# Tile 0's second matrix product: chunks 8 to 15 in three float32r products where plain float32 stood

## The chip, the cores and the metric

The kernel runs on one core of one Trainium2 chip. The metric is the device time in microseconds (us) of one execution. A core has five engines that each work through their own queue in order: PE (TensorE, matrix products, with weight loads counted apart as PEld), DVE (VectorE), ACT (ScalarE), POOL (GpSimd) and SP (which issues the transfers here).

## The reference

```
x = attention(q, k, v)        # 4 batches x 8 heads x 576 rows x 64, window of 128, slopes by head
h = x @ moe_w_in              # 2304 x 512 times 512 x 2048
r = max(h, 0)
g = s * (r * r) + b
y = g @ moe_w_out             # 2304 x 2048 times 2048 x 512
a, c = y @ moe2_w1, y @ moe2_w2
out = ((a * c) @ moe2_w3) @ moe2_w_out
```

## The kernel before

The 2304 rows are cut into six tiles of 384 (`TT`), and the hidden width of 2048 into sixteen chunks of 128 (`NC1`). For each tile and chunk the kernel makes the first product into `hp` (`mlp_h`), takes relu and square on ACT into `r` (`mlp_relu`, `mlp_g`), and adds the second product, chunk by chunk, into four accumulators `acc` (`mlp_x`, one per 128 output columns). Attention runs one head per slot beside it, some heads ahead: scores `s` on PE, mask and minimum `ns` on DVE (L311, then L320), exponentials on ACT (L334), their sums `sm` on DVE (L344, L345), normalizing `pr` on POOL (L347), a transpose `tp` on PE (L368), the split of it `pp` on ACT and DVE (L380, L381), a selection `pt` on POOL (L384), and the product with the values, `pv`, on PE (L421).

Two ways of multiplying are used. Tiles 1 to 5 use float32r, with each operand split into a high part and the rest: an operand x becomes xh = round(x) and xl = x - xh, and a product is three products, high by high, high by rest, rest by high (`PASSES`). Tile 0 uses plain float32 operands without a split, in both products of the first layer (L482 and L534). A plain float32 product is one instruction in the program and two rows in the trace: L534 has 64 in the program (16 chunks of 4) and 128 in the trace. A float32r product is one row.

The weights arrive as 8-byte numbers and are decoded by `decode`: ACT reads the upper words into a scratch tile `z` (L98), DVE does a shift and two merges (L100, L103, L109). The scratch pool has two buffers. With `plain` the last merge writes the finished weight `wz` to a tile of its own and so frees `z`; without it the merge writes into `z`, and ACT and POOL then split `z` into the two halves of a weight tile `w` (L121, L122). All 32 weight chunks of the first layer (16 of w_in, 16 of w_out, by turns) are decoded plain before and during tile 0. Those of tile 0 that are plain are split afterwards for tiles 1 to 5: `mlp_x` puts them on the list `unsplit`, and `split_some` takes four in each slot from slot 7 on (`weight_split`: ACT copy L131, subtraction L132 on POOL and on DVE by turns). The pool of weight tiles has 33 buffers for 32 chunks, so such splits follow each other through one spare buffer.

The order in which each engine meets its instructions is set when the program is built: the framework's scheduler starts from the order of the source and moves instructions by a timeline of its own, engine by engine. On the chip each engine's queue is then strictly in order.

Of the kernel before, what the change touches and what calls it, by code (L numbers as in the profile page):

```python
# [8 lines left out]
F32 = mybir.dt.float32  # L9
F32R = mybir.dt.float32r  # L10
U32 = mybir.dt.uint32
BF16 = mybir.dt.bfloat16
AF = mybir.ActivationFunctionType
ALU = mybir.AluOpType
# [7 lines left out]
P = 128  # L22
TT = 384
# [9 lines left out]
EARLY = H  # L33
EX = 2
AHEAD = 3
PASSES = ((0, 0), (0, 1), (1, 0))


@with_exitstack
def kernel(  # L40
    ctx: ExitStack, tc: tile.TileContext, qk0, qk, v, relm, w_in, w_out, s, b, w1, w2, w3T, wo2, qsc, v0, out
):
    nc = tc.nc
# [3 lines left out]
    wp = ctx.enter_context(tc.tile_pool(name="wp", bufs=2 * NC1 + 1))  # L47
    xp = ctx.enter_context(tc.tile_pool(name="xp", bufs=2 * KD))
    gp = ctx.enter_context(tc.tile_pool(name="gp", bufs=2))
# [36 lines left out]
    def decode(raw, pool, tag, done, free=None, plain=False):  # L86

        z = zp.tile([P, DM], F32, tag="z", name="z")  # L90
        if raw.dtype == F32:
            nc.vector.tensor_copy(out=z, in_=raw)
            yield
        else:
            zu = z.bitcast(U32)
            wu = raw.bitcast(U32).rearrange("p (n t) -> p n t", t=2)
            wf = raw.bitcast(F32).rearrange("p (n t) -> p n t", t=2)
            nc.scalar.activation(out=z, in_=wf[:, :, 1], func=AF.Copy, scale=2.0 ** -112)  # L98
            yield
            nc.vector.tensor_scalar(  # L100
                out=zu, in0=zu, scalar1=3, scalar2=None, op0=ALU.logical_shift_left
            )
            nc.vector.scalar_tensor_tensor(  # L103
                out=zu, in0=wu[:, :, 1], scalar=0x80000000, in1=zu,
                op0=ALU.bitwise_and, op1=ALU.bitwise_or,
            )
            if plain:
                z = pool.tile([P, DM], F32, tag=tag, name="wz")
            nc.vector.scalar_tensor_tensor(  # L109
                out=z.bitcast(U32), in0=wu[:, :, 0], scalar=29, in1=zu,  # L110
                op0=ALU.logical_shift_right, op1=ALU.bitwise_or,
            )
            if plain:
                done(z)
                yield
                return
        if free:
            free()
        yield
        w = pool.tile([P, 2, DM], F32R, tag=tag, name="w")  # L120
        nc.scalar.activation(out=w[:, 0, :], in_=z, func=AF.Copy)  # L121
        nc.gpsimd.tensor_tensor(  # L122
            out=w[:, 1, :], in0=z, in1=w[:, 0, :].bitcast(F32), op=ALU.subtract
        )
        done(w)
        yield
# [64 lines left out]
    def load_raws(n):  # L191
        for _ in range(n):
            if nraw[0] < len(raws):
                raw_load(*raws[nraw[0]])
                nraw[0] += 1

    def tick(n=1):
        for _ in range(n):
            if todo:
                need[0] += 1  # L200
                if len(raws) == 2 * NC1 and need[0] + AHEAD > nraw[0]:
                    load_raws(need[0] + AHEAD - nraw[0])
                flight.append(todo.pop(0)())
# [267 lines left out]
    wi, wo, hps, gs, x2acc, unsplit = {}, {}, {}, {}, {}, []  # L471
# [6 lines left out]
    def mlp_h(t, c):  # L478
# [9 lines left out]
        n = 0  # L488
        for l, r in PASSES:
            for k in range(KD):  # L490
# [14 lines left out]
    def mlp_g(t, c):  # L505
        rt = gs[t, c]
        nc.scalar.activation(out=rt[:, :TT], in_=rt[:, :TT], func=AF.Square)
        if t == 0:
            nc.vector.memset(rt[:, TT:], 1.0)
            return  # L510
        gh = gp.tile([P, TT], F32R, tag="gh", name="gh")
        nc.scalar.activation(out=gh, in_=rt[:, :TT], func=AF.Copy)  # L512
        gs[t, c] = rt, gh

    def mlp_gl(t, c):
        if t == 0:
            return
        rt, gh = gs[t, c]
        gl = gp.tile([P, TT], F32R, tag="gl", name="gl")
        nc.vector.tensor_tensor(  # L520
            out=gl, in0=rt[:, :TT], in1=gh.bitcast(F32), op=ALU.subtract
        )
        gs[t, c] = gh, gl

    def mlp_x(t, c):
        g = gs.pop((t, c))
        w = TT + EX if t == 0 else TT
        if c == 0:
            for m in range(KD):
                x2acc[m] = ps_acc.tile([P, w], F32, tag="acc", name="acc")  # L530
        for m in range(KD):
            ms = slice(m * P, (m + 1) * P)
            if t == 0:
                nc.tensor.matmul(  # L534
                    out=x2acc[m], lhsT=wo[c][:, ms], rhs=g,
                    start=(c == 0), stop=(c == NC1 - 1),
                )
                continue
            for n, (l, r) in enumerate(PASSES):
                nc.tensor.matmul(  # L540
                    out=x2acc[m], lhsT=wo[c][:, l, ms], rhs=g[r],
                    start=(c == 0 and n == 0), stop=(c == NC1 - 1 and n == 2),
                )
        if t == 0:
            unsplit.extend(((wi, c), (wo, c)))
        if c == NC1 - 1:
            for m in range(KD):
                z = xp.tile([P, TT], F32, tag="x", name="ev")
                bm = bcol[:, m:m + 1]
                if t == 0:  # L550
                    nc.vector.tensor_scalar(
                        out=bm, in0=x2acc[m][:, TT:TT + 1], scalar1=b_sb[:, 0:1], scalar2=None,
                        op0=ALU.mult,
                    )
                if m % 2:
                    nc.vector.tensor_scalar(
                        out=z, in0=x2acc[m][:, :TT], scalar1=s_sb[:, 0:1], scalar2=bm,
                        op0=ALU.mult, op1=ALU.add,
                    )
                else:  # L560
                    nc.scalar.activation(
                        out=z, in_=x2acc[m][:, :TT], func=AF.Identity, scale=s_sb[:, 0:1], bias=bm
                    )
                nc.sync.dma_start(out=x2d[t][m], in_=z)
# [4 lines left out]
    def w3_unit(ig, j, accs):  # L569
# [3 lines left out]
        for i in range(4):  # L573
            for n, (l, r) in enumerate(PASSES):
                nc.tensor.matmul(  # L575
# [28 lines left out]
    def mlp2_ab(t, c):  # L604
        ps = []
        for w in (wa, wb):
            d = ps_rot.tile([P, TT], F32, tag="rot", name="ab")
            n = 0
            for l, r in PASSES:
                for k in range(KD):  # L610
# [19 lines left out]
    def mlp2_o(t, c):  # L630
        p = ps2.pop((t, c))
        for i in range(NB):
            if c == 0:
                oacc[i] = ps_acc.tile([P, DM], F32, tag="acc", name="acc")
            cs = slice(i * P, (i + 1) * P)
            for n, (l, r) in enumerate(PASSES):
                nc.tensor.matmul(  # L637
# [13 lines left out]
    for c in range(NC1):  # L651
        for d, src in ((wi, w_in[c]), (wo, w_out[c * P:(c + 1) * P, :])):
            raw = wp.tile([P, DM], src.dtype, tag="w", name="raw")
            raws.append((raw, src))
            todo.append(
                lambda raw=raw, d=d, c=c: decode(
                    raw, wp, "w", lambda w: d.__setitem__(c, w), plain=True
                )
            )
    att_load(0)  # L660
# [32 lines left out]
    def slot(n, m):  # L693
# [17 lines left out]
        if mlp:  # L711
            mlp_relu(*seq[1])
            mlp_g(*seq[1])
        if s1:
            att_min(n)
        if mlp:
            mlp_gl(*seq[1])
            pre_tick(more)
        if q > 0:
            mlp_x(*seq[0])  # L720
# [21 lines left out]
        if mlp:  # L742
            mlp_g(*seq[2])
            if v2 is not None:
                att_v(v2)
                att_x(v2)
            mlp_gl(*seq[2])
        if v2 is not None:
            att_xt(v2)
        if mlp:  # L750
            tick()
            pre_tick(more)
            mlp_x(*seq[1])
# [11 lines left out]
    n, m = EARLY, 0  # L765
# [44 lines left out]
    for m in range(KD):  # L810
        x2_split(0, m)
    mlp_x(NTILE - 1, NC1 - 1)
    accs = []
    while fresh[0] < npre[0]:
# [91 lines left out]
```

## Time and profile before

| | |
|---|---|
| time, median of 3 runs | 911.92 us (906.9 to 913.98) |
| the profiled execution's own time | 907.65 us |
| its span, first to last instruction | 905.9 us |
| mean granted TensorE clock | 0.990 of full speed |
| PE busy | 887.2 us (98%), 4833 rows |
| DVE, ACT, POOL busy | 484.6, 453.4, 340.4 us |

The profiled execution lies 4.3 us below the median, and 1.75 us of its time lie outside its span. PE is busy nearly throughout, so the questions are what PE has to do in the stretch that the change touches (about 60 to 190 us from the start of the span), and where in it PE waits.

### The profile page before, as it was taken

What the parts mean: (1) busy time and instruction counts of PE and PEld (TensorE: products, weight loads), DVE (VectorE), ACT (ScalarE), POOL (GpSimd) and SP (SyncE); (2) the same over time, 40 slices, a digit from 0 to 9 for tenths busy, and PEclk for the clock granted to TensorE, in tenths of its full rate; (3) what the DMA queues carried; (4) which work ended last, traced back from release to release, by engine and by line L of the source; (5) the groups of instructions that cost most, each with busy time, mean ns of one, the idle gap of its engine ahead of it and who ended that gap; (6) DMA issues with size and microseconds to landing.
All of it is one profiled execution on the core that took longest, in us unless ns stands there. A gap on an engine that the chain in (4) does not pass through costs nothing.

```text
span 905.9 us, 13384 instructions
## 1 busy us (share of the span) xinstructions
PE 887.2 (98%) x4833; PEld 805.5 (89%) x4836; DVE 484.6 (53%) x1012; ACT 453.4 (50%) x1052; POOL 340.4 (38%) x376
## 2 busy tenths in 40 slices
PE   8989989999999999999999999999999999999997
PEld 4756656999999999999999999899999999999996
DVE  5998866766688887788752621482211212121212
ACT  5756667776767787777754543342212121121211
POOL 0154687775567686777641301240101001010000
PEclk8989999999999999999999999999999999999999
DMA  8974211213334455445326962130201002000000
GB/s 312 304 283 166 100 64 46 85 59 112 99 127 166 169 201 170 145 157 181 117 94 224 385 261 84 56 116 1 71 1 35 36 1 70 1 36 1 35 1 36
DMA packets 37219, 104.38 MB, mean 115 GB/s; under 512 B 4512, under 2 KB 10656, under 8 KB 37152
## 3 DMA queue, kind: packets, MB, share of 16 engines
q1 hardware_dynamic: 37152, 103.52, 33.0%
q8 instruction: 38, 0.62, 0.3%
q14 instruction: 29, 0.24, 0.1%
HBM read 82.00 MB, written 21.50 MB: 114 GB/s over the span
## 4 chain that ended last, share of the span: by engine, by line
PE 85%; DVE 6%; issue 2%; POOL 2%; ACT 2%; DMA 2%; SPq 1%; DVEq 0%; ACTq 0%; POOLq 0%
PE ab L611 21%; PE acc L540 17%; PE hp L491 17%; PE acc L637 11%; PE hp L482 3%; PE acc L534 3%; PE pv L421 3%; PE w3a L575 2%; DVE z L103 2%; PE tp L368 1%; PE s L298 1%; PE s L297 1%; PE s L292 1%; DMA vraw<-v 1%; DVE z L100 1%
## 5 line engine op out<-in xcount | busy, mean ns | idle before, releaser
L611 PE MATMUL ab<-x,w 128*128 128x384 f32 x1152 | 208.3, 335 | 0.0
L611 PEld LDWEIGHTS ab<-x,w 128*128 128x128 f32 x1152 | 201.8, 188 | 4.3
L491 PE MATMUL hp<-x,w 128*128 128x384 f32 x960 | 186.2, 340 | 0.9 <-DVE pp L381 0.9
L540 PE MATMUL acc<-gh,w 128*128 128x384 f32 x640 | 177.3, 339 | 0.0
L491 PEld LDWEIGHTS hp<-x,w 128*128 128x128 f32 x960 | 167.6, 188 | 1.4 <-DVE pp L381 1.1
L625 DVE TENSOR_TENSOR a<-ab,a 128x384 f32<-128x384 f32 x48 | 26.7, 557 | 197.7 <-PE ab L611 179.8
L540 PEld LDWEIGHTS acc<-gh,w 128*128 128x128 f32 x640 | 115.3, 188 | 0.3
L540 PE MATMUL acc<-gl,w 128*128 128x384 f32 x320 | 108.6, 339 | 1.5 <-DVE gl L520 1.5
L599 POOL TENSOR_TENSOR x<-x,x 128x384 fp32r<-128x384 f32 x24 | 25.6, 1093 | 203.8 <-ACT x L598 191.9
L347 POOL TENSOR_SCALAR pr<-pr,sm 128x128 f32<-128x128 f32 x120 | 63.5, 543 | 88.3 <-DVE sm L345 34.7
L637 PE MATMUL acc<-w3o,ph 128*128 128x512 f32 x288 | 89.9, 394 | 0.0
L624 ACT ACTIVATE a<-ab 128x384 f32<-128x384 f32 x48 | 23.6, 492 | 131.7 <-PE ab L611 131.7
L259 POOL TENSOR_TENSOR kb<-qkraw,ka 128x512 fp32r<-128x512 f32 x40 | 56.2, 1404 | 71.4 <-ACT ka L258 71.3
L384 POOL TENSOR_SCALAR_AFFINE_SELECT pt<-pp 128x768 fp32r<-128x768 f32 x80 | 77.2, 986 | 7.0 <-PE pv L421 6.5
L520 DVE TENSOR_TENSOR gl<-r,gh 128x384 fp32r<-128x384 f32 x80 | 57.8, 723 | 33.6 <-ACT gh L512 32.4
L311 DVE CUSTOM_DVE_ANT_0 ns<-s,relm_sb 128x256 f32<-128x256 f32 (+1 forms) x144 | 52.9, 412 | 39.2 <-PE s L298 30.1
L626 ACT ACTIVATE ph<-a 128x384 fp32r<-128x384 f32 x48 | 25.2, 525 | 92.7 <-DVE a L625 92.7
L502 ACT ACTIVATE r<-hp 128x384 f32<-128x384 f32 x96 | 46.5, 486 | 49.6 <-PE hp L491 43.5
L540 PEld LDWEIGHTS acc<-gl,w 128*128 128x128 f32 x320 | 60.3, 188 | 2.3 <-DVE gl L520 2.2
L637 PEld LDWEIGHTS acc<-w3o,ph 128*128 128x128 f32 x288 | 53.4, 187 | 8.9
L637 PE MATMUL acc<-w3o,pl 128*128 128x512 f32 x144 | 56.5, 396 | 0.2 <-DVE pl L627 0.2
L334 ACT ACTIVATE pr<-pr,mn 128x128 f32<-128x128 f32 x120 | 46.8, 392 | 19.3 <-DVE pr L320 16.6
(89 smaller groups left out, 1423.4 us busy)
## 6 DMA issues: line engine op xcount, KB each, us to landing
qkraw<-qk SPq DMA_DIRECT2D x45, 448.0 KB, 3.3
late<-st SPq DMA_DIRECT2D x23, 512.0 KB, 3.4
w<-late SPq DMA_DIRECT2D x23, 512.0 KB, 7.1
raw<-w_in SPq DMA_DIRECT2D x16, 512.0 KB, 7.1
raw<-w_out SPq DMA_DIRECT2D x16, 512.0 KB, 6.7
raw<-w SPq DMA_DIRECT2D x16, 512.0 KB, 5.2
st<-w3T SPq DMA_DIRECT2D x15, 512.0 KB, 3.8
vraw<-v SPq DMA_DIRECT2D x20, 256.0 KB, 2.6
```

The source lines that it names most:

```text
L259: nc.gpsimd.tensor_tensor(out=kl, in0=k_r, in1=k.bitcast(F32), op=ALU.subtract)
L311: nc.vector.tensor_tensor_reduce(out=n[:, i, cs], in0=dst[i][:, cs], in1=relm_sb[:, VARIANT.get(t * NB + i, 0), cs], scale=2.0 ** -(h + 1) ...
L334: nc.scalar.activation(out=e[:, i, :], in_=e[:, i, :], func=AF.Exp, scale=-1.0, bias=mn[:, i:i + 1], accum_out=sm[:, i:i + 1],)
L347: nc.gpsimd.tensor_scalar(out=e[:, i, :], in0=e[:, i, :], scalar1=sm[:, i:i + 1], scalar2=1.0, op0=ALU.mult, op1=ALU.mult,)
L384: nc.gpsimd.affine_select(out=o[:, :, :, e, :], in_=pp.bitcast(F32), pattern=[[0, 2], [0, NB], [sign, P]], compare_op=op, fill=0.0, base=0 ...
L421: nc.tensor.matmul(out=d, lhsT=l, rhs=r, start=(n == 0), stop=(n == len(mms) - 1), skip_group_check=True)
L491: nc.tensor.matmul(out=hp, lhsT=wi[c][:, l, k * P:(k + 1) * P], rhs=xT[t, k][:, r, :], start=(n == 0), stop=(n == 3 * KD - 1),)
L502: nc.scalar.activation(out=rt[:, :TT], in_=hps.pop((t, c)), func=AF.Relu)
L520: nc.vector.tensor_tensor(out=gl, in0=rt[:, :TT], in1=gh.bitcast(F32), op=ALU.subtract)
L540: nc.tensor.matmul(out=x2acc[m], lhsT=wo[c][:, l, ms], rhs=g[r], start=(c == 0 and n == 0), stop=(c == NC1 - 1 and n == 2),)
L611: nc.tensor.matmul(out=d, lhsT=w[c][:, l, k * P:(k + 1) * P], rhs=x2[t, k][:, r, :], start=(n == 0), stop=(n == 3 * KD - 1),)
L637: nc.tensor.matmul(out=oacc[i], lhsT=p[l][:, cs], rhs=w3o[c][:, r, :], start=(c == 0 and n == 0), stop=(c == NC2 - 1 and n == 2),)
```

## The change

For tile 0 a constant `PLAIN = 8` parts the second product. Chunks 0 to 7 stay as they were. For chunks 8 to 15 the weight of w_out is decoded with its split at once (L121 and L122 of `decode`, on ACT and POOL), the squared activations are split into `gh` and `gl` as in the other tiles (ACT L512, DVE L520, now 386 columns wide with the two columns of ones), and the second product is made of three float32r products. These eight weight chunks no longer go on the list `unsplit`, which therefore holds 24 entries and not 32.

```diff
+PLAIN = 8
@@ mlp_g
         if t == 0:
             nc.vector.memset(rt[:, TT:], 1.0)
-            return
-        gh = gp.tile([P, TT], F32R, tag="gh", name="gh")
-        nc.scalar.activation(out=gh, in_=rt[:, :TT], func=AF.Copy)
+            if c < PLAIN:
+                return
+        w = TT + EX if t == 0 else TT
+        gh = gp.tile([P, TT + EX], F32R, tag="gh", name="gh")
+        nc.scalar.activation(out=gh[:, :w], in_=rt[:, :w], func=AF.Copy)
         gs[t, c] = rt, gh
@@ mlp_gl
-        if t == 0:
+        if t == 0 and c < PLAIN:
             return
+        w = TT + EX if t == 0 else TT
         rt, gh = gs[t, c]
-        gl = gp.tile([P, TT], F32R, tag="gl", name="gl")
+        gl = gp.tile([P, TT + EX], F32R, tag="gl", name="gl")
         nc.vector.tensor_tensor(
-            out=gl, in0=rt[:, :TT], in1=gh.bitcast(F32), op=ALU.subtract
+            out=gl[:, :w], in0=rt[:, :w], in1=gh[:, :w].bitcast(F32), op=ALU.subtract
         )
@@ mlp_x
-            if t == 0:
+            if t == 0 and c < PLAIN:
                 nc.tensor.matmul(
                     out=x2acc[m], lhsT=wo[c][:, ms], rhs=g,
...
-                    out=x2acc[m], lhsT=wo[c][:, l, ms], rhs=g[r],
+                    out=x2acc[m], lhsT=wo[c][:, l, ms], rhs=g[r][:, :w],
...
         if t == 0:
-            unsplit.extend(((wi, c), (wo, c)))
+            unsplit.extend(((wi, c), (wo, c)) if c < PLAIN else ((wi, c),))
@@ where the decodes are listed
-                    raw, wp, "w", lambda w: d.__setitem__(c, w), plain=True
+                    raw, wp, "w", lambda w: d.__setitem__(c, w), plain=d is wi or c < PLAIN
```

In the changed file the lines stand 1 to 4 lower: L98 becomes L99, L121 L122, L122 L123, L347 L348, L502 L503, L507 L508, L534 L538, L540 L544. Up to about 61 us of the trace the order of every engine is unchanged, and from early in tile 1 on (row 444 of 1819 on PE) PE's order is again the old one.

The first place is ACT's queue at the decodes of chunk 9 of w_in and chunk 9 of w_out, at about 61 us. The names in brackets are the engines (and transfers) for which an instruction waits. Before:

```order
L507 ACTIVATE r<-r 128x384 [waits Activation_49]
L98 ACTIVATE z<-raw 128x512 [waits DMAHW4_49,DVE_49]
L98 ACTIVATE z<-raw 128x512 [waits DMAHW0_49,DVE_49]
L98 ACTIVATE z<-raw 128x512 [waits DMAHW1_49,DVE_49]
L98 ACTIVATE z<-raw 128x512 [waits DMAHW3_49,DVE_49]
L502 ACTIVATE r<-hp 128x384 [waits PE_49,Activation_49]
```

After:

```order
L508 ACTIVATE r<-r 128x384 [waits Activation_49]
L99 ACTIVATE z<-raw 128x512 [waits DMAHW4_49,DVE_49]
L122 ACTIVATE w<-z 128x512 [waits DVE_49]
L99 ACTIVATE z<-raw 128x512 [waits DMAHW0_49,DVE_49]
L99 ACTIVATE z<-raw 128x512 [waits DMAHW1_49,Pool_49]
L503 ACTIVATE r<-hp 128x384 [waits PE_49]
L122 ACTIVATE w<-z 128x512 [waits DVE_49]
L508 ACTIVATE r<-r 128x384 [waits Activation_49]
L99 ACTIVATE z<-raw 128x512 [waits DMAHW3_49,DVE_49]
L99 ACTIVATE z<-raw 128x512 [waits DMAHW4_49,Pool_49]
```

The ACT copies of the splits have moved in between the first steps of the decodes, and every other first step (the one that takes over the scratch buffer of a split weight) waits for POOL and not for DVE.

The second place is POOL's queue at the same time. Before:

```order
L347 TENSOR_SCALAR pr<-pr,sm 128x128 x3
L384 AFFINE_SELECT pt<-pp 128x6x128 x2
L259 TENSOR_TENSOR kb<-qkraw,ka 128x512
L347 TENSOR_SCALAR pr<-pr,sm 128x128 x3
L384 AFFINE_SELECT pt<-pp 128x6x128 x2
```

After:

```order
L348 TENSOR_SCALAR pr<-pr,sm 128x128 x3
L385 AFFINE_SELECT pt<-pp 128x6x128 x2
L123 TENSOR_TENSOR w<-z,w 128x512 x2
L260 TENSOR_TENSOR kb<-qkraw,ka 128x512
L123 TENSOR_TENSOR w<-z,w 128x512
L348 TENSOR_SCALAR pr<-pr,sm 128x128 x3
L123 TENSOR_TENSOR w<-z,w 128x512
L385 AFFINE_SELECT pt<-pp 128x6x128 x2
```

Four of the eight new subtractions stand among the attention work of two heads, the first of them behind the selection `pt`.

The third place is PE's queue at chunk 8. Before:

```order
L482 MATMUL hp<-xe,wz 128x384 x4
L534 MATMUL acc<-r,wz 128x386 x2
L421 MATMUL pv<-pt,vv 128x256 x2
L421 MATMUL pv<-pt,vv 128x128 x2
L421 MATMUL pv<-pt,vv 128x256 x2
L421 MATMUL pv<-pt,vv 128x128 x2
L534 MATMUL acc<-r,wz 128x386 x2
```

After:

```order
L483 MATMUL hp<-xe,wz 128x384 x4
L422 MATMUL pv<-pt,vv 128x256 x2
L422 MATMUL pv<-pt,vv 128x128 x2
L422 MATMUL pv<-pt,vv 128x256 x2
L422 MATMUL pv<-pt,vv 128x128 x2
L298 MATMUL s_1174<-ka,qa 128x256
L299 MATMUL s_1174<-kb,qa 128x256
L298 MATMUL s_1174<-ka,qa 128x256
L544 MATMUL acc<-gh,w 128x386 x4
L544 MATMUL acc<-gl,w 128x386
L544 MATMUL acc<-gh,w 128x386
L544 MATMUL acc<-gl,w 128x386
```

The four plain products of chunk 8 have become twelve, four of them with `gl`, and they stand later, between the scores of the next head.

## Rows read from the trace of the kernel before

**Rows 1.** The page: the span, and PE's busy time with its share and rows.

```profile
span 905.9 us, 13384 instructions
...
PE 887.2 (98%) x4833; PEld 805.5 (89%) x4836; DVE 484.6 (53%) x1012; ACT 453.4 (50%) x1052; POOL 340.4 (38%) x376
```

**Rows 2.** Stretches: us; busy of PE, PEld, DVE, ACT, POOL; PE's clock; DMA share; GB/s.

```profile
60.00:70.00 10.00, 10.00 (x30) 5.80 (x30) 9.86 (x17) 5.08 (x10) 5.58 (x6) 0.95 0.75 266
...
110.00:120.00 10.00, 7.97 (x38) 5.29 (x37) 6.18 (x16) 6.45 (x17) 10.00 (x11) 1.00 0.18 59
120.00:130.00 10.00, 8.01 (x26) 4.99 (x27) 6.12 (x15) 7.23 (x19) 8.40 (x11) 0.83 0.18 61
...
200.00:250.00 50.00, 50.00 (x318) 49.81 (x317) 33.49 (x76) 34.00 (x89) 30.15 (x40) 1.00 0.31 99
```

**Rows 3.** The chain that ended last, 0 to 170 us: start, us, what.

```profile
71.66 2.59 PE acc L534 x8
...
122.65 4.28 PE hp L482 x8
...
167.87 2.08 PE acc L540 x12
```

**Rows 4.** Groups by line and shape: count | busy us, mean ns | idle before.

```profile
L540 PE MATMUL acc<-gh,w 128*128 128x384 f32 x640 | 177.3, 339 | 0.0
...
L520 DVE TENSOR_TENSOR gl<-r,gh 128x384 fp32r<-128x384 f32 x80 | 57.8, 723 | 33.6 <-ACT gh L512 32.4
...
L534 PE MATMUL acc<-r,wz 128*128 128x386 f32 x128 | 44.7, 489 | 0.0
...
L512 ACT ACTIVATE gh<-r 128x384 fp32r<-128x384 f32 x80 | 41.5, 518 | 1.8 <-PE acc L540 0.8
...
L122 POOL TENSOR_TENSOR w<-z,w 128x512 fp32r<-128x512 f32 x17 | 22.9, 1350 | 63.3 <-ACT w L121 63.3
...
L132 POOL TENSOR_TENSOR w<-wz,w 128x512 fp32r<-128x512 f32 x16 | 20.9, 1308 | 4.8 <-ACT w L131 4.7
...
L131 ACT ACTIVATE w<-wz 128x512 fp32r<-128x512 f32 x32 | 20.1, 627 | 16.0 <-POOL w L132 11.9 <-DVE w L132 4.1
...
L132 DVE TENSOR_TENSOR w<-wz,w 128x512 fp32r<-128x512 f32 x16 | 13.1, 816 | 16.8 <-ACT w L131 16.7
```

**Rows 5.** PE in order of time: start, us, what, count [idle before <-releaser].

```profile
90.97 0.49 PE L368 MATMUL tp<-ident,pr 128*128 128x128 f32 x3
...
114.38 1.14 PE L421 MATMUL pv<-pt,vv 128*128 128x256 f32 x8 [0.89 <-POOL vv L275]
...
121.60 0.33 PE L368 MATMUL tp<-ident,pr 128*128 128x128 f32 x1 [2.74 <-POOL pr L347]
122.32 0.33 PE L368 MATMUL tp<-ident,pr 128*128 128x128 f32 x1 [0.39 <-POOL pr L347]
...
164.80 2.36 PE L491 MATMUL hp<-x,w 128*128 128x384 f32 x12 [0.93 <-DVE pp L381]
```

**Rows 6.** ACT in order of time: first steps of two decodes.

```profile
61.78 0.68 ACT L98 ACTIVATE z<-raw 128x512 f32<-128x512 f32 x1 [0.28 <-DVE wz L109]
64.49 0.70 ACT L98 ACTIVATE z<-raw 128x512 f32<-128x512 f32 x1 [2.03 <-DVE wz L109]
```

**Rows 7.** POOL in order of time: a selection, and the normalizing of a later head.

```profile
63.88 2.58 POOL L384 TENSOR_SCALAR_AFFINE_SELECT pt<-pp 128x768 fp32r<-128x768 f32 x2
...
88.18 1.06 POOL L347 TENSOR_SCALAR pr<-pr,sm 128x128 f32<-128x128 f32 x3 [2.30 <-DVE sm L345]
```

**Rows 8.** DVE in order of time: the same merge twice, then the mask of a later head.

```profile
64.38 1.35 DVE L103 SCALAR_TENSOR_TENSOR z<-raw,z 128x512 uint32<-128x512 uint32 x1
...
67.37 0.69 DVE L103 SCALAR_TENSOR_TENSOR z<-raw,z 128x512 uint32<-128x512 uint32 x1
...
84.43 0.41 DVE L311 CUSTOM_DVE_ANT_0 ns<-s,relm_sb 128x256 f32<-128x256 f32 x1
```

**Rows 9.** Who waited for whom: us in total, times, longest; whole span.

```profile
ACT z L98 <- POOL w L122: 7.9, 12, 1.4
```

## The prediction

> **What bounds the kernel now.** I read the page first: PE is busy for 98% of a span of 905.9 us [rows 1], so only what PE does or waits for can count. The profile warns that the ends of matrix products are modelled, so I take PE's cost from starts that follow each other, and then ask stretch by stretch whether PE is full. From tile 1 on it is: 318 rows in 50 us, clock 1.00, no idle time [rows 2]. In the chain of waits twelve float32r products of the second matrix product advance it by 2.08 us, 0.173 us each; eight rows of the plain product by 2.59 us, 0.324 us each [rows 3]. Tile 0 ends at about 165 us [rows 5], and before that PE is not always full: of 110 to 130 us it has only 16 busy, and POOL is the one that is full (10.00 and 8.40 of 10) [rows 2]. PE in order of time names the waits: 0.89, 2.74 and 0.39 us for POOL, 4.0 together, and 0.93 us for DVE at the first full product of tile 1 [rows 5]. [...] Earlier, at 60 to 70 us, PE never waits but DVE is busy 9.86 of 10 us [rows 2]: the decodes run there at DVE's pace, with attention squeezed in between.
>
> **The change on PE.** Plain products: 8 chunks of 4, two rows each, 64 rows of the 128 [rows 4], by 0.324 us: 20.7 us go. In their place come 8 x 4 x 3 = 96 float32r products; two columns on 384 are half a per cent, so 0.174 us each: 16.7 us come. PE's own work falls by 4.0 us. Weight loads go from 64 to 96; in the stretch from 200 us on as many loads as products run beside them with PE at 0.173 us, so they cost nothing of their own, and without that cover the products would show it there.
>
> **On the other engines.** Per chunk ACT gets one copy of 0.52 us and DVE one subtraction of 0.72 us [rows 4], 4.1 and 5.8 us in all. The eight splits of w_out are no new work for ACT (0.63 us each either way), but they come earlier, and all on POOL: 8 x 1.35 us, while of the later splits four on POOL (1.31 us) and four on DVE (0.82 us) go [rows 4]. So POOL gets 10.8 - 5.2 = 5.6 us more and DVE 5.8 - 3.3 = 2.5 us more. None of it is PE's, so it costs only where PE waits for it. No transfer is added, and two rows of SP change places. What counts is order and time, so I walk the new orders with the durations of the old rows.
>
> **The decodes, 61 to 95 us.** The scratch buffer of a split weight is free only after POOL's subtraction. The first of them stands behind the selection that ran from 63.88 us for 2.58 us [rows 7]; it ends at 66.46 + 1.35 = 67.8 us. The decode step that takes this buffer started at 64.49 us and waited for DVE [rows 6]; now it starts at 67.8, 3.3 us later, and ACT holds everything behind it (relu and square of chunk 2 among it; walking on, the relu of chunk 5 is the first that PE waits for, 0.5 us). The first step before it (61.78 us, [rows 6]) also moves, to about 64.2, since it now waits for the DVE merge of the weight before. DVE, full until now, stands still for about 2 us until the late step arrives. The same handover recurs with chunks 9, 10 and 11, where POOL is freer: 0.4 to 0.7 us each. How such a wait looks is in the trace already, at the late decodes of the second layer's weights, which take the split path: 7.9 us over 12 times, 0.66 us each, 1.4 at most [rows 9]. Those have nothing else in POOL's queue, so they are the lower bound and 3.3 us is the upper. By the mask of the head that stood at 84.43 us [rows 8] I am 4 us late, and two more decode steps of DVE stand before the operations behind it; its normalizing on POOL, at 88.18 us before [rows 7], comes at 93.3 and ends at 95. PE needs it for the transposes that stood at 90.97 us [rows 5] and is itself 1 us late by then: it waits about 3 us. Bounds: 0 (the 1.7 us of slack between 89.24 and 90.97, and DVE catching up) and 5.
>
> **The second product, 110 to 165 us.** Its last eight passes per chunk wait for relu, square, then `gh` and `gl`, where only relu and square stood. The new orders put more between them: first decode steps and an L121 copy that itself waits for DVE, and at chunk 11 four L131 copies in a row ahead of the relu, which follow each other through one spare buffer and two engines (0.63 + 1.31 and 0.63 + 0.82 us, twice: 6.8 us). Walking it, PE waits for `gh` or `gl` 2.4 + 0.7 us at chunk 9, 2.1 at chunk 10, 1.2 at 11, 1.3 at 15, and not at 8 and 12 to 14: 7.7 us. The trace of before has this wait rarely (1.5 us over 320 products of `gl`, [rows 4]) because there the order leaves room; that is the lower bound, 0.04 us a chunk, and the upper is 2.3 us at each of eight, 18. I take 7.7, since chunk by chunk the order decides it.
>
> **What goes.** The 4.0 us of waits for POOL and the 1.7 us of the low clock at 113 to 126 us: they come from POOL's queue there, and the new order has the same attention work behind other things, later. I count them as gone, since the waits I named are all that my walk finds, and put a fall of the clock back in: with gaps of 2 to 3 us at 92 and 115 us it falls at least once, 1.7 us by the row that shows it. The 0.93 us at the end of tile 0 I leave.
>
> **Sum.** -4.0 (products) -5.7 (old waits and clock) + 0.5 (chunk 5 late for its relu) + 3 + 7.7 + 1.7 = +3.2 us. The tiles after it are as full as before and add nothing. The profiled execution takes 907.65 us and would take 910.9; it was 4.3 us under the median of 911.92, so for a median I say **915 us**, which is within 1%, about the least that a measurement of this kernel can tell from no change.
>
> [...] Where POOL selects from 63.88 to 66.46 us, the DVE merge L103 took 1.35 us, and 0.69 at 67.37 with POOL idle [rows 7, 8]: 0.66 us more for one overlap. [...]
>
> **The rivals.**
> (a) The new waits do not form: DVE catches up between heads and the relu is early enough. Then only the gains are left, with the end of tile 0: -4.0 - 5.7 - 0.9 = -10.6, 901 us. For it: DVE and ACT are busy only 6 to 7 of 10 us from 110 us on [rows 2]. Against: at 60 to 70 us DVE has no room. Chance 0.10. Between it and the forecast, half of the new waits: -4 to -1, 909 us: 0.16.
> (b) Slower: the chain relu, square, `gh`, `gl` is late at every chunk, since ACT stays one queue of decodes and splits behind. Then 18 instead of 7.7, and the clock falls twice: +3.2 + 10.3 + 1.7 = +15, 927 us. It decides from the point where the relu of a chunk is so late that its square ends less than 1.2 us (`gh` 0.52, `gl` 0.72) before PE reaches its passes. Chance 0.12.
> (c) [...] Chance 0.07.
> (d) That PE's rows do not change as said is excluded by the order: 32 instructions gone, 96 come. The forecast keeps 0.55.
>
> **How the numbers follow.** Faster by over 1% (below 902.8) needs nearly all of (a): 0.08. Slower by over 1% (above 921): most of (b), and an edge of the forecast and of (c): 0.13. Within 1%: 0.79. The range has to leave out no more than 2 in 10: it runs from just above the whole of (a), 902, to just short of (b), 926.
>
> **What would show it.** Right: 96 rows of 386 columns at 0.174 us between starts; the decode step after the first split starting at about 67.8 us and waiting for POOL; DVE idle about 2 us there; PE waiting some 3 us for `pr` near 92 us and 1 to 2.5 us for `gh` or `gl` at chunks 9, 10, 11 and 15; tile 1 full from about 168 us. Wrong: a PE without waits from 60 to 165 us (a), or waits at each of the chunks (b). What would upset the reckoning altogether is a second stretch of low clock, or an order on DVE that lets the masks of a head slip by a whole slot.

## The result, and the profile after

The changed kernel takes 916.16 us (median of 6 runs, 914.93 to 926.04); the kernel before, run beside it, takes 906.83 us (median of 6, 904.34 to 913.98). The ratio is 1.0117 with a 95% interval from 1.0080 to 1.0153: slower by 1.2%, 9 us by the medians and 11 by the ratio, where 3 were forecast. The time lies in the range, and only 1.2 us from the 915 that was named; that nearness is luck. The first three runs of before, from which the forecast starts, had a median 5 us higher than all six, and the change costs 6 to 7 us more than forecast; the two errors cancel. By the ratio the outcome is one to which the prediction gave 0.13, slower by over 1%, though the interval reaches below 1%. All ratios below are against the kernel before, over the undisturbed runs alone; they are no quotients of the medians and can differ from these by up to 0.4%.

The profiled execution took 915.31 us, of which the span is 913.6; before it was 907.65 and 905.9 [rows 1]. The page of after, its span and the line of busy times:

```profile
span 913.6 us, 13470 instructions
...
PE 889.4 (97%) x4865; PEld 815.3 (89%) x4868; DVE 493.0 (54%) x1016; ACT 454.9 (50%) x1060; POOL 350.5 (38%) x380
```

PE has the 32 rows more that the change gives it, and 7.7 us more of span. The two executions happen to reach the first scores beyond 65 us at the same time (70.49 us before, 70.47 after), so all of the loss lies behind that. Stretches of after (us; busy of PE, PEld, DVE, ACT, POOL; PE's clock; DMA share; GB/s):

```profile
60.00:70.00 10.00, 9.75 (x31) 5.88 (x32) 8.96 (x13) 4.83 (x12) 7.01 (x8) 1.00 0.82 299
110.00:120.00 10.00, 7.24 (x38) 5.62 (x37) 8.50 (x24) 7.23 (x19) 5.23 (x7) 1.00 0.16 48
120.00:130.00 10.00, 8.15 (x36) 6.53 (x34) 8.67 (x21) 5.60 (x16) 10.00 (x10) 0.83 0.24 72
130.00:140.00 10.00, 8.81 (x30) 6.64 (x30) 3.84 (x8) 4.90 (x13) 6.65 (x9) 0.66 0.14 46
200.00:250.00 50.00, 50.00 (x316) 49.83 (x315) 29.74 (x69) 32.31 (x85) 27.50 (x39) 1.00 0.24 78
```

Against [rows 2]: DVE is no longer full at 60 to 70 us, because it now stands and waits; PE has gaps at 110 to 130 us as before; and the granted clock, 0.83 in one stretch before, is 0.83 and then 0.66, falling after the wait at 118 us (1.00 at 118 to 120 us, 0.52 at 120 to 122) and again after those at 129 to 131 us (1.00 at 128 to 130, 0.50 at 132 to 136). The stretch from 200 us on is as full as it was. PE of after in order of time, the rows with a wait, and some of chunk 8's float32r rows and one at the low clock (start, us, what, count [idle before <-releaser]):

```profile
70.47 0.58 PE L298 MATMUL s<-ka,qa 128*128 128x256 f32 x1
...
84.83 2.86 PE L538 MATMUL acc<-r,wz 128*128 128x386 f32 x8 [0.32 <-ACT r L508]
...
91.03 2.85 PE L483 MATMUL hp<-xe,wz 128*128 128x384 f32 x8 [2.46 <-DVE mn L312]
...
95.50 0.85 PE L369 MATMUL tp<-ident,pr 128*128 128x128 f32 x3 [0.92 <-DVE xf L454]
...
113.87 0.34 PE L544 MATMUL acc<-gh,w 128*128 128x386 f32 x1
...
114.94 0.34 PE L544 MATMUL acc<-gh,w 128*128 128x386 f32 x1
...
118.37 0.97 PE L544 MATMUL acc<-gh,w 128*128 128x386 f32 x4 [2.54 <-ACT gh L515]
...
129.09 0.97 PE L544 MATMUL acc<-gh,w 128*128 128x386 f32 x4 [1.85 <-ACT gh L515]
...
131.24 0.69 PE L544 MATMUL acc<-gl,w 128*128 128x386 f32 x1 [1.19 <-DVE gl L524]
...
134.19 4.22 PE L483 MATMUL hp<-xe,wz 128*128 128x384 f32 x8
...
173.60 0.39 PE L298 MATMUL s<-ka,qa 128*128 128x256 f32 x1 [0.56 <-ACT r L503]
...
174.54 0.39 PE L298 MATMUL s<-ka,qa 128*128 128x256 f32 x1 [0.20 <-ACT r L503]
...
175.46 0.97 PE L544 MATMUL acc<-gh,w 128*128 128x384 f32 x4 [0.42 <-ACT gh L515]
```

The new products are as cheap as said: 113.87 to 114.94 us is six steps, 0.178 us each. The waits sum to 10.5 us where [rows 5] has 4.95. The wait of 2.46 us at 91.03 us is for a buffer in PSUM (the memory whose tiles this kernel's products write) of the rotating pool: the mask of a head (L312, `mn`) must have read its scores before `hp` can take the buffer. ACT, POOL and DVE of after, one fence each, on how that mask came to be late:

```profile
67.92 0.68 ACT L99 ACTIVATE z<-raw 128x512 f32<-128x512 f32 x1 [2.28 <-POOL w L123]
...
106.03 0.67 ACT L99 ACTIVATE z<-raw 128x512 f32<-128x512 f32 x1 [4.17 <-POOL w L123]
```

```profile
64.35 2.13 POOL L385 TENSOR_SCALAR_AFFINE_SELECT pt<-pp 128x768 fp32r<-128x768 f32 x2
66.45 1.43 POOL L123 TENSOR_TENSOR w<-z,w 128x512 fp32r<-128x512 f32 x1
...
76.58 1.70 POOL L123 TENSOR_TENSOR w<-z,w 128x512 fp32r<-128x512 f32 x1 [1.29 <-ACT w L122]
80.61 2.97 POOL L348 TENSOR_SCALAR pr<-pr,sm 128x128 f32<-128x128 f32 x3 [2.33 <-ACT z L99]
```

```profile
66.80 1.64 DVE L104 SCALAR_TENSOR_TENSOR z<-raw,z 128x512 uint32<-128x512 uint32 x1
...
77.07 1.63 DVE L321 TENSOR_TENSOR pr<-ns 128x384 f32<-128x384 f32 x1
...
90.21 0.41 DVE L312 CUSTOM_DVE_ANT_0 ns<-s,relm_sb 128x256 f32<-128x256 f32 x1
...
92.41 0.55 DVE L321 TENSOR_TENSOR pr<-ns 128x384 f32<-128x384 f32 x1
```

The first split's subtraction stands behind the selection, and ACT takes over its `z` at 67.92 us (67.8 was forecast). DVE waits for ACT there, and besides, three operations of DVE that begin while a POOL subtraction runs last longer than elsewhere: L104 1.64 us beside the one at 66.45 and 0.68 at 69.58, L101 0.69 beside the one at 70.41 and 0.43 at 68.63, L321 1.63 beside the one at 76.58 and 0.55 at 92.41, where POOL had stood idle and began its next operation at 92.62. The mask that stood at 84.43 us [rows 8] now stands at 90.21, 5.8 us later. PE was ready at 88.57 (91.03 less the wait) and waited 2.46 us, so a mask some 3.3 us late would have cost nothing.

### The profile page after: what moved, and what is told of

Its sections match the earlier page's. It is cut to its first block, busy times and chain, and to the rows that moved or that the text cites. A ratio compares the mean times of both kernels' runs of the same rounds, so it can differ in the third digit from the quotient of the medians.

```text
span 913.6 us, 13470 instructions
## 1 busy us (share of the span) xinstructions
PE 889.4 (97%) x4865; PEld 815.3 (89%) x4868; DVE 493.0 (54%) x1016; ACT 454.9 (50%) x1060; POOL 350.5 (38%) x380
## 4 chain that ended last, share of the span: by engine, by line
PE 82%; DVE 8%; ACT 4%; issue 3%; POOL 2%; DMA 1%; SPq 0%; DVEq 0%; POOLq 0%; ACTq 0%
PE ab L615 21%; PE acc L544 18%; PE hp L492 17%; PE acc L641 11%; PE pv L422 3%; PE w3a L579 2%; PE hp L483 2%; PE acc L538 1%; DVE z L104 1%; PE tp L369 1%; PE s L298 1%; PE s L299 1%; DVE z L101 1%; PE s L293 1%; DVE qa L245 1%
## 5 line engine op out<-in xcount | busy, mean ns | idle before, releaser
L544 PE MATMUL acc<-gh,w 128*128 128x384 f32 (+1 forms) x704 | 197.9, 343 | 4.8 <-ACT gh L515 4.8
L544 PEld LDWEIGHTS acc<-gh,w 128*128 128x128 f32 x704 | 127.9, 190 | 5.9 <-ACT gh L515 5.4
L544 PE MATMUL acc<-gl,w 128*128 128x384 f32 (+1 forms) x352 | 121.4, 345 | 1.7 <-DVE gl L524 1.4
L348 POOL TENSOR_SCALAR pr<-pr,sm 128x128 f32<-128x128 f32 x120 | 64.2, 549 | 78.9 <-ACT z L147 26.7
L524 DVE TENSOR_TENSOR gl<-r,gh 128x384 fp32r<-128x384 f32 (+1 forms) x88 | 63.0, 716 | 32.1 <-ACT gh L515 30.7
L385 POOL TENSOR_SCALAR_AFFINE_SELECT pt<-pp 128x768 fp32r<-128x768 f32 x80 | 73.7, 942 | 13.2 <-PE pv L422 6.7
L312 DVE CUSTOM_DVE_ANT_0 ns<-s,relm_sb 128x256 f32<-128x256 f32 (+1 forms) x144 | 53.0, 412 | 37.7 <-PE s L299 29.1
L503 ACT ACTIVATE r<-hp 128x384 f32<-128x384 f32 x96 | 46.4, 485 | 50.6 <-PE hp L492 47.3
L544 PEld LDWEIGHTS acc<-gl,w 128*128 128x128 f32 x352 | 67.1, 190 | 3.5 <-DVE gl L524 3.1
L123 POOL TENSOR_TENSOR w<-z,w 128x512 fp32r<-128x512 f32 x25 | 35.7, 1431 | 72.0 <-ACT w L122 72.0
```

The lines of the kernel that those rows point to most:

```text
L123: nc.gpsimd.tensor_tensor(out=w[:, 1, :], in0=z, in1=w[:, 0, :].bitcast(F32), op=ALU.subtract)
L312: nc.vector.tensor_tensor_reduce(out=n[:, i, cs], in0=dst[i][:, cs], in1=relm_sb[:, VARIANT.get(t * NB + i, 0), cs], scale=2.0 ** -(h + 1) ...
L348: nc.gpsimd.tensor_scalar(out=e[:, i, :], in0=e[:, i, :], scalar1=sm[:, i:i + 1], scalar2=1.0, op0=ALU.mult, op1=ALU.mult,)
L385: nc.gpsimd.affine_select(out=o[:, :, :, e, :], in_=pp.bitcast(F32), pattern=[[0, 2], [0, NB], [sign, P]], compare_op=op, fill=0.0, base=0 ...
L503: nc.scalar.activation(out=rt[:, :TT], in_=hps.pop((t, c)), func=AF.Relu)
L524: nc.vector.tensor_tensor(out=gl[:, :w], in0=rt[:, :w], in1=gh[:, :w].bitcast(F32), op=ALU.subtract)
```

## The experiments

The theories on record: A, the handover of `z` (buffers free too late); B, load (more work on ACT and DVE, whoever waits); C, the clock alone; E, POOL's longer queue; D, POOL and DVE hold each other up; and, from x9 on, F, that DVE's lateness up to the mask decides. The scheduler orders each kernel anew, so a small difference between two kernels is also one of order. Spans are compared from the first scores beyond 65 us on, since executions differ by over 5 us in when they reach these: before 905.9 - 70.49 = 835.4 us, after 843.1.

**x1, no wait for gh and gl.** In `mlp_x`:

```diff
-                    out=x2acc[m], lhsT=wo[c][:, l, ms], rhs=g[r][:, :w],
+                    out=x2acc[m], lhsT=wo[c][:, l, ms],
+                    rhs=(wo[PLAIN][:, r, :w] if t == 0 else g[r][:, :w]),
```

> Left out: in tile 0 the float32r products of chunks 8 to 15 take the split weight of chunk 8 as their moving operand and not gh and gl; the two copies and subtractions are still made, but nobody waits for them. Against the kernel before (the changed kernel is at +9 us by its median, +7.7 by its profile). Theory A (late handoffs): PE's 5.6 us of waits for gh and gl at chunks 9 and 10 are gone, and with these gaps the second fall of the clock, 3.4 us: 0 us, between -3 and +3; the 3.4 us of waits for the mask and the normalizing near 91 to 96 us stay. Theory B (load): the new work on ACT, DVE and POOL makes everything late whoever waits for it, so PE waits at hp or tp in their place: +5 to +9. Theory C (clock alone): the clock falls at other gaps too, so the waits go and the fall stays: +3 to +5.

910.72 us, ratio 1.0031 (0.9999 to 1.0062), from the first scores on 837.8 us. Some 5 of the 8 us by the spans are gone, as theory A had it, but not all: the wait for the mask is still there, 2.5 us. Theory C comes near the time too (+3 to +5), but not the clock: it is 1.00 from 70 to 160 us and 0.83 once, at 160 to 170, so the fall went from where the waits went and is no larger than before. This operand also spares PE the wait for relu and square, so x1 shows what the whole chain up to the product costs, not `gh` and `gl` alone.

**x6, the early split alone.** The counterpart: no `gh`, no `gl`, but a product that still needs the square. `mlp_g` and `mlp_gl` return early for all of tile 0, and in `mlp_x`:

```diff
-            if t == 0 and c < PLAIN:
+            if t == 0:
                 nc.tensor.matmul(
-                    out=x2acc[m], lhsT=wo[c][:, ms], rhs=g,
+                    out=x2acc[m], lhsT=wo[c][:, ms] if c < PLAIN
+                    else wo[c][:, 0, ms].bitcast(F32), rhs=g,
```

> Left out: the product of chunks 8 to 15 stays plain float32, on the squared activations, with the high half of the weight alone (its rest is made, but not multiplied); there is no gh and no gl. What is left of the change is the early split with its handover of z. Against the kernel before. Theory A: the waits near 91 to 96 us stay (3.4 us) and the products save nothing: +3 to +7, without a wait for gh or gl and with one fall of the clock. Theory B (load): ACT and DVE are spared 8 x (0.52 + 0.6) us: -1 to +2.

917.45 us, ratio 1.0124 (1.0070 to 1.0178), from the first scores on 10.1 us longer than before: more than theory A's 3 to 7, and theory B falls. PE of x6 in order of time:

```profile
89.97 2.85 PE L483 MATMUL hp<-xe,wz 128*128 128x384 f32 x8 [2.45 <-DVE mn L312]
...
128.71 3.53 PE L537 MATMUL acc<-r,w 128*128 128x386 f32 x6 [3.66 <-ACT r L508]
```

The wait for the mask is the same to 0.01 us, and at 128.71 us, chunk 10, PE waits 3.66 us for the square, in the place where the changed kernel waits 1.85 + 1.19 us for `gh` and `gl`. So there the wait is not the price of the two new operations: what comes before them is late. At chunk 9, where the changed kernel waits 2.54 us, x6 has no wait, so for that one x6 alone doesn't decide.

**x2, the early subtractions on DVE.** In `decode`, with `early` set for the first layer's chunks:

```diff
-        nc.gpsimd.tensor_tensor(
+        (nc.vector if early else nc.gpsimd).tensor_tensor(
             out=w[:, 1, :], in0=z, in1=w[:, 0, :].bitcast(F32), op=ALU.subtract
```

> The eight early subtractions of w_out's split go from POOL to DVE, so that the scratch buffer comes free without standing behind POOL's selections. Against the kernel before. Theory A (handover): no first decode step waits for POOL in tile 0; the waits for the mask and the normalizing near 91 to 96 us (3.4 us) shrink to under 1: +4 to +6. Theory B (load on DVE): DVE has no room between 60 and 95 us and gets 8 x 0.82 = 6.6 us more, so the mask is as late or later: +8 to +12. [...]

907.95 us, ratio 0.9999 (0.9968 to 1.0030): the whole loss is gone, more than any theory had said, and theory B's "8 to 12" is refuted. From 74.66 us, its first scores, the span is 835.4 us, as before. Who waited for whom in x2 (us in total, times, longest), DVE from 68 to 95 us, then PE from 75 to 200:

```profile
DVE z L101 <- ACT z L99: 0.3, 1, 0.3
```

```profile
PE tp L369 <- POOL pr L348: 2.2, 1, 2.2
PE tp L369 <- DVE xf L454: 0.9, 1, 0.9
...
PE acc L544 <- ACT gh L515: 0.4, 1, 0.4
```

In the same stretch of the changed kernel (64 to 91 us) DVE waited for `z` 2.3 us, 5 times. In x2 the mask stands 16.5 us behind the first scores (13.9 before, 19.7 after): late, but within PE's room, and no wait for it is left. `gh` is hardly waited for, although its operations are all there.

**x5, a shadow on POOL.** This parts the handover from the mere work of POOL. x2 with, behind each early subtraction:

```diff
+            nc.gpsimd.tensor_tensor(
+                out=shadow[0][:, :DM], in0=w[:, 0, :].bitcast(F32),
+                in1=relm_sb[:, :2].rearrange("p v q -> p (v q)"), op=ALU.subtract,
+            )
```

> The kernel of x2 (early subtractions on DVE), and on POOL, at the eight places where they stood, a subtraction of the same size (high half minus a constant, into a tile nobody reads). The scratch buffer comes free from DVE, as in x2, while POOL reads SBUF as in the changed kernel. The output is unchanged. Against the kernel before (x2: 0; the changed kernel: +9). Theory A (the handover of z): nobody waits for the shadow, so as x2: -2 to +2. Theory D (POOL and DVE hold each other up): DVE operations between 60 and 95 us last 1.0 to 1.7 us again where x2 has 0.4 to 0.8, up to 0.66 each, so +3 to +6, and the waits for the mask come back. Theory E (POOL's queue): the normalizing stands behind eight operations of 1.35 us more; PE waits for pr instead: +2 to +4.

914.04 us, ratio 1.0075 (1.0043 to 1.0107), span from the first scores (69.52 us) 841.6 us. Up to the mask the order of DVE is that of x2, operation by operation, and behind it that of DVE and ACT differs by a few rows; `z` comes from DVE in both, yet some 6 us are back. Theory A, as the whole cause, falls, and theory D comes nearest, a little beyond its +3 to +6. POOL, DVE and PE of x5:

```profile
66.21 1.69 POOL L127 TENSOR_TENSOR shadow<-w,relm_sb 128x512 f32<-128x512 f32 x1
69.60 1.66 POOL L127 TENSOR_TENSOR shadow<-w,relm_sb 128x512 f32<-128x512 f32 x1 [1.69 <-ACT w L122]
...
76.12 1.52 POOL L127 TENSOR_TENSOR shadow<-w,relm_sb 128x512 f32<-128x512 f32 x1 [1.35 <-ACT w L122]
...
83.00 1.66 POOL L127 TENSOR_TENSOR shadow<-w,relm_sb 128x512 f32<-128x512 f32 x1
```

```profile
66.71 1.48 DVE L101 TENSOR_SCALAR z<-z 128x512 uint32<-128x512 uint32 x1
...
70.04 1.77 DVE L123 TENSOR_TENSOR w<-z,w 128x512 fp32r<-128x512 f32 x1
...
75.95 0.56 DVE L252 SCALAR_TENSOR_TENSOR qa<-qkraw,qa 64x384 fp32r<-64x384 f32 x1
76.53 1.52 DVE L328 TENSOR_TENSOR pr<-ns 128x384 f32<-128x384 f32 x1
...
78.59 0.68 DVE L123 TENSOR_TENSOR w<-z,w 128x512 fp32r<-128x512 f32 x1
...
83.43 1.77 DVE L123 TENSOR_TENSOR w<-z,w 128x512 fp32r<-128x512 f32 x1
...
90.02 0.41 DVE L319 CUSTOM_DVE_ANT_0 ns<-s,relm_sb 128x256 f32<-128x256 f32 x1
```

```profile
90.84 4.54 PE L490 MATMUL hp<-xe,wz 128*128 128x384 f32 x8 [2.72 <-DVE mn L319]
```

DVE's own subtraction takes 0.68 us at 78.59, with POOL idle; the one that begins 0.44 us into a shadow takes 1.77 and ends 0.55 us after the shadow (71.81 against 71.26). The mask is 20.5 us behind the first scores, and PE waits 2.72 us for it. The theory E, that the normalizing comes late behind POOL's longer queue, has little: that wait is 2.6 us at its longest here and 2.2 in x2. Summed from 7 us before the first scores up to the mask, the time of DVE's operations above the short ones (the lowest quarter) of their own form is 3.6 us before, 3.5 in x2, 6.2 in the changed kernel and 7.9 here. The same 45 operations begin in that stretch in x2 and in x5, and they last 4.3 us longer in x5, which accounts for the 4.0 us by which its mask is later. Four of them begin beside the first four shadows, at 66.71, 70.04, 76.53 and 83.43 us, and last about 1.05 us longer each, 4.2 us in all.

**x9, four on DVE, four on POOL.** x2 with `nc.vector if early and c < 12 else nc.gpsimd`.

> The early subtractions of chunks 8 to 11 on DVE as in x2, those of chunks 12 to 15 on POOL as in the changed kernel. Against the kernel before (x2: 0, the changed kernel: +9, x5: +7). Theory F (what counts is DVE in the full stretch up to the mask 20 us after the first scores beyond 65 us; there PE has about 3.4 us of room): the same there as x2, so no wait for that mask, and -1 to +3. Theory A (the handover wherever it is): ACT is held again by a first decode step that waits for POOL (4.17 us in the changed kernel), with gh late behind it: +4 to +6.

910.91 us, ratio 1.0054 (1.0025 to 1.0083): halfway. ACT and PE of x9:

```profile
103.29 0.69 ACT L99 ACTIVATE z<-raw 128x512 f32<-128x512 f32 x1 [3.60 <-POOL w L123]
```

```profile
115.66 0.98 PE L544 MATMUL acc<-gh,w 128*128 128x386 f32 x4 [2.55 <-ACT gh L515]
...
125.42 0.97 PE L544 MATMUL acc<-gh,w 128*128 128x386 f32 x4 [2.21 <-ACT gh L515]
...
128.20 0.58 PE L544 MATMUL acc<-gl,w 128*128 128x386 f32 x1 [1.82 <-DVE gl L524]
```

No wait for the mask, so the first four subtractions made that one; but the waits for `gh` and `gl` are all back, 6.6 us, with ACT held for POOL at 103 us as in the changed kernel at 106 us. So the last four on POOL make these. It is mostly the handover that does it and not POOL's work: in x5, where POOL has four shadows at these places but `z` comes from DVE, the waits for `gh` and `gl` in tile 0 are 0.71 and 0.91 us (PE's order is another there, so the size is approximate). Theory F holds for the first half and is too narrow for the second, where theory A's +4 to +6 is met.

**x3 and x11, a third scratch buffer and its control.** x3 sets `zp` to 3 buffers and, for room, `kb` to 1; x11 sets `kb` to 1 only.

> Three scratch buffers z where there are two (and one buffer of kb where there are two, to make room). No work changes place by hand, though the scheduler orders anew. Against the kernel before. Theory A (handover): the first decode step behind a split no longer waits for POOL; the 3.4 us of waits near 91 to 96 us go, and the waits for gh and gl shrink where ACT was held by such a step (4.17 us at 106 us): 0 to +5. Theory B (load): same work, same time: +7 to +9.

> The control to x3: the changed kernel with one buffer of kb and still two scratch buffers. Against the kernel before (x3: +7, the changed kernel: +9). If the third scratch buffer is worth something: +9 to +13, above x3. If x3's gain came from the new order alone: +5 to +7, as x3.

x3: 913.12 us, ratio 1.0072 (1.0041 to 1.0104). x11: 909.29 us, ratio 1.0033 (1.0001 to 1.0065). The control is no slower than x3, so the third buffer earned nothing, although ACT's waits for POOL from 55 to 135 us fell from 6.9 us to this (waits view of x3):

```profile
ACT z L99 <- POOL w L123: 2.3, 2, 1.7
```

That speaks against the handover as the cause, but weakly: x3 has another order from 13 us on. x11 is also a warning. Like x3 it moves no work from one engine to another, and it comes out below the changed kernel by 0.8% of the time, from the first scores on by 5.9 us (837.2). Up to 82 us its DVE and ACT have the changed kernel's order, and DVE waits for `z` as much (2.1 us against 2.3). But the mask stands ahead of six decode steps that the changed kernel puts before it, 13.3 us behind the first scores, and PE doesn't wait for it. So order alone is worth that much here: it decides whether DVE's lateness falls on an operation that PE needs. The pair x2 and x5, whose DVE order is the same up to the mask, therefore carries more than any other difference.

**x4, x8, x7: how many chunks.** `PLAIN` is 12 with POOL (x4), 12 with DVE (x8) and 4 with DVE (x7).

> PLAIN is 12: four chunks are changed and not eight, all decoded behind the stretch in which DVE is full. Against the kernel before. Theory A: no handover wait before 95 us, no gh wait at chunks 9 and 10; products -1.8 us, old waits for POOL partly stay: -3 to +3. Theory B (load, by the chunk): half of what eight cost: +4 to +5.

> x2 with PLAIN 12: four chunks in float32r, early subtractions on DVE. Against the kernel before; x4, the same with POOL, was level with it. Theory A: its four splits come behind the full stretch, so the engine hardly matters: as x4, -2 to +2. Theory D (POOL and DVE hold each other up wherever they meet): 1 to 3 us better than x4.

> x2 with PLAIN 4: twelve chunks in float32r, all early subtractions on DVE. Against the kernel before. Theory A: products -5.4 us (12 chunks at 0.45), waits as in x2 or a little more: -3 to +1. Theory B (load on DVE): the decodes begin to be split before 60 us, where attention of the first heads runs too; DVE gets 3 us more in the full stretch: +2 to +6.

x4: 910.22 us, ratio 0.9998 (0.9964 to 1.0031). x8: 911.93 us, 1.0029 (0.9998 to 1.0060). x7: 922.92 us, 1.0157 (1.0112 to 1.0201). Four late chunks cost nothing and gain nothing that can be told, on either engine (from the first scores on 834.7 us in x4, 835.7 in x8); theory D had x8 better than x4, which it is not. Twelve with DVE are the slowest of all. Theory B had the direction, but its +2 to +6 is far below the 14 us that the ratio gives. Stretches of x7:

```profile
80.00:90.00 10.00, 7.33 (x31) 6.05 (x30) 9.87 (x23) 6.27 (x16) 6.52 (x8) 0.83 0.56 192
90.00:100.00 10.00, 4.97 (x23) 3.80 (x21) 9.84 (x20) 5.46 (x15) 5.02 (x5) 0.77 0.23 69
```

DVE is full and PE half idle at 90 to 100 us. That eight subtractions, as in x2, are about what DVE can still take is a reading of these two doses and not shown: in x7 the order is another as well.

**x10, filling the gap.** The changed kernel with this ahead of chunk 9's loop in `mlp_x`:

```diff
+            for _ in range(10):
+                nc.tensor.matmul(out=fill[:, :P], lhsT=ident, rhs=ident, start=True, stop=True)
```

> The changed kernel with ten small plain products (identity by identity, 2.2 us by the rows of the transposes) put ahead of chunk 9's second product, where PE waited 2.54 us for gh and the granted clock fell afterwards. Their result is used by nobody. Against the kernel before (the changed kernel: +9). If the gap brings the fall of the clock: the fall behind it goes, 1.7 us, while the fill itself lies in the gap: +6 to +8. If the clock falls without that gap as well: +9 to +11.

919.33 us, ratio 1.0126 (1.0082 to 1.0170). The scheduler put the fill behind chunk 9's products, at 124.3 us, into the gap ahead of chunk 10, so it did not test the gap that was meant. It tells something else. Stretches of x10:

```profile
120.00:130.00 10.00, 8.20 (x50) 6.65 (x50) 9.12 (x20) 7.32 (x22) 10.00 (x10) 1.00 0.25 72
130.00:140.00 10.00, 10.00 (x52) 7.81 (x51) 4.65 (x14) 6.69 (x15) 7.71 (x11) 1.00 0.24 73
```

The clock stayed full where it was 0.83 and 0.66, and from the first scores on the kernel takes 842.6 us, where the changed kernel takes 843.1. The fill lies in the gap of 1.85 us that it was not meant for, and 1.6 us of waits for `gh` and `gl` at 156 to 162 us are new, so this too is another order.

**x12, x1 and x2 together.**

> x1 and x2 together: early subtractions on DVE, and the products of chunks 8 to 15 without waiting for gh and gl. Left out: as in x1, the moving operand of those products is the split weight of chunk 8. Against the kernel before. Theory F: neither cost of the change is left, so the saving of the products shows, 3.6 us, with part of the old waits: -5 to -2. If something else comes late in their place (the normalizing, the transposes): -1 to +2.

908.08 us, ratio 1.0026 (0.9996 to 1.0055): the saving of the products does not show even so. PE of x12, two of its rows:

```profile
153.34 2.85 PE L483 MATMUL hp<-xe,wz 128*128 128x384 f32 x8 [1.16 <-ACT r L503]
...
166.00 2.03 PE L492 MATMUL hp<-x,w 128*128 128x384 f32 x10 [2.28 <-POOL x L466]
```

Relu and POOL's part of `x` are late now; all waits from the first scores to 125 us later sum to 6.7 us. What PE saves, it waits for later.

## Where the prediction was right, and where it was off

**The products** (-4.0 us). The rows came as said, 96 of them, 0.178 us between starts inside a chunk. The saving was mis-sized. Counted from each row's start to the start of the next, waits left out, the 64 plain rows that go took 19.6 us in the kernel before, 0.306 each: 0.324 is what they take where `hp` follows, and they take about 0.29 where scores or `pv` follow. The 96 that come took 18.0 us in x2, where next to no wait falls among them. That is 1.6 us less, not 4.0.

**The decodes** (+0.5 and +3 us). Place and size were right: the chunk 5 wait is 0.32 us, the two near 91 and 95 us are 2.46 and 0.92; 3.7 in all for 3.5. The operand was not: PE waits for the mask through a PSUM buffer and for `xf`, not for `pr`. And the way there had a part that the sum left out: the mask is 5.8 us late, not 4. DVE's waits for `z` explain 2.3 us of it, and operations that POOL stretches 2.6 (6.2 less 3.6). It is not more work: from 7 us before the first scores up to the mask 41 operations of DVE begin in either kernel. 0.9 us are left, among them 0.5 of DVE's waits for other operations.

**The second product** (+7.7 us). 2.54 us at chunk 9 (forecast 2.4 + 0.7), 1.85 + 1.19 at chunk 10 (2.1), nothing at 11 and 15 (1.2 and 1.3): 5.6 us, and at the start of tile 1 another 1.2 where the old 0.93 was. Here the reason was wrong, more than the size. I put it down to the longer chain relu, square, `gh`, `gl` and to decode steps and copies that the order puts between them. x6 has a wait at chunk 10 without `gh` and `gl`, x2 has them without the waits, and x9 brings all back with four subtractions on POOL. The handover that I priced at "0.4 to 0.7 us each" for chunks 9 to 11 I did not price at all for 12 to 15, where it held ACT for 4.17 us. A slip besides: 1.5 us over 320 products of `gl`, four a chunk, are 0.02 us a chunk and not 0.04; it only moves the lower bound.

**What goes** (-5.7 us, and +1.7 put back). This term failed by its size. The old waits for POOL do go (none of the 4.0 us is left behind 70 us), but the clock's 1.7 us was counted as gone and once as back, while the stretches of after from 70 us on add up to 1.7 + 3.4 = 5.1 us below full clock. The 1.7 us for one fall is what eight plain rows at 122.65 us took above eight at 71.66, 4.28 against 2.59 us [rows 3]; the clock was 0.83 there [rows 2]. That a gap of 2 to 3 us brings a fall was my estimate from that one, and it held at one of the two places: after the 2.46 us at 91 us the clock stayed 1.00 up to 120 us, after the 2.54 at 118 it fell.

The sum with measured terms is -1.6 for the products, 10.5 - 4.95 = +5.5 for the waits, 5.1 - 1.7 = +3.4 for the clock: +7.3 us, against 7.7 by the spans. The sum describes where the time is, and not its causes: the clock's share isn't shown to be one, since x10 has none of it and is as slow.

**The rivals.** (c), to which I gave 0.07, took the 0.66 us by which one DVE merge lasted longer beside POOL [rows 7, 8] for each of the eight new subtractions, 5.3 us. x5 shows such overlaps as what makes the mask late (7.9 us of stretched DVE time against 3.5 in x2), so it should have been a term of the sum and no rival beside it: I had the rows for it. What in the chip makes POOL and DVE hold each other up no run shows. The 5.3 us come near the 6 us by which x5 lies behind x2, but in part by luck: up to the mask there are four overlaps of about 1.05 us in x5, and in the changed kernel 0.96, 0.27 and 1.07 us beside three of the four subtractions. I took the four subtractions that come after 95 us to cost nothing; x9, where just these four stand on POOL and the kernel is 0.5% slower than before, refutes that, though their way is mostly the handover. (a), no new waits, was wrong. (b) had the clock fall twice, as it did, but not a wait at every chunk.

**What stays open.** Whether the change must cost anything: x11, with the same work on the same engines, is 0.3% slower than the kernel before and not 1.2%, by its order alone. Whether PE's work is the bound in tile 0 at all. x12 has neither cost and gains nothing, x4 gains nothing, and a full clock in x10 gains nothing; all three fit a stretch whose pace DVE, ACT and POOL set. Taking products out of the kernel before would tell, and was not tried. How much of x2's gain is DVE's freedom from POOL and how much its order is bounded by x5 from one side only, since x11 shows that order alone can move the time by as much. And x9 and x5 part the handover from POOL's work behind the mask only with different orders of PE.

## What to carry to other kernels

A saving on the fullest engine need not show in a stretch where another engine is full; before an operation is moved there, read what DVE and POOL do in just that stretch, and cost the operation on both, since each lengthened the other here (a subtraction on DVE from 0.68 to 1.77 us in x5, one on POOL from 1.35 to as much as 1.73). The room between a late engine and the one that needs it (here 3.3 us up to one mask) decides whether an added microsecond is free or paid in full. Between none of these versions and the kernel before is there a gain to keep: x2 and x4 are level with it.

## What the runs showed of the hardware

A DVE subtraction of two operands in SBUF (the memory of the kernel's other working tiles) lasted 0.68 us by itself and 1.77 beside a POOL subtraction (x5, 78.59 and 70.04 us), and POOL's own went from 1.35 us on the mean [rows 4] to 1.43 to 1.73 in the stretch of the changed kernel where DVE is busy (66.45 to 85.28 us). Not only operations with two inputs were stretched: the shift L101, with one, took 0.43 us alone and up to 1.50 beside POOL (68.63 and 87.57 us of the changed kernel), while the mask, which reads PSUM, took 0.41 us either way (90.21 us alone, 74.08 beside POOL). Beside POOL's normalizing it was the other way round: at 80.6 to 83.6 us of the changed kernel DVE's merges kept 0.68 to 0.77 us, and the three normalizing operations took 2.97 us, where they took 1.06 at 94.91. And profiled executions differ by 5.6 us in when they reach the first scores beyond 65 us (69.0 us in x10, 70.47 in the changed kernel, 74.63 in x1), though PE's order is the same in all three up to there, so spans of two profiles compare only from a common instruction on.
